# Second MoE of a fused attention and two-MoE kernel: one branch per pair of experts, and a second small product split by feature quarters

## The chip, the cores and the metric

The kernel runs on one core of a Trainium2 chip. The metric is the device time of one execution in microseconds (us); the time before is the median of three runs, 1041.02 us (1039.25 to 1041.88). Two times that lie within 0.3% of each other, some 3.1 us, are not told apart here.

## The reference, cut to what matters

A linear attention feeds a dense MoE (every token through all eight experts), and its output `x` (1152 tokens of 512 features) feeds a second MoE in which each token goes to one expert. Only that last part is touched:

```python
expert_idx = np.argmax(x @ w_gate, axis=1)          # one expert of E = 8 for each token
gate_w = probs[np.arange(N), expert_idx]
for i in range(N):                                   # capacity = 288 rows for each expert
    e = expert_idx[i]
    if counts[e] < capacity:
        disp[e, counts[e]] = x[i]; pos[i] = counts[e]; counts[e] += 1; keep[i] = True
h = np.maximum(np.einsum('ecd,edf->ecf', disp, w1), 0.0)   # D = 512, F = 1024
y = np.einsum('ecf,efd->ecd', h, w2)
out[i] = gate_w[i] * y[expert_idx[i], pos[i]]        # for the rows kept, else 0
```

How many rows an expert holds is known only when the kernel runs.

## The kernel before

The first 90% of the kernel (attention, first MoE, routing) ends with a scatter by GpSimd: each token's row of the tile `acc` (512 features and the gate weight and token number behind them) goes to its slot of the DRAM tensor `disp` (line 723). The rows of the first four experts' first 32 slots are also built on chip, as `xT`.

Then the second MoE runs expert by expert, `for e in range(E)`. It treats an expert's 288 slots in two parts.

- **The small part**, the first 32 slots, is always computed. `first_small` multiplies the 32 rows with w1 (16 matmuls, four of them side by side in the array's columns, each for a quarter of the 1024 features; 32 instructions in the trace, since a float32 matmul is issued as two). `relu_small` takes the result through ScalarE into `g`. `turn_small` transposes `g` on TensorE, VectorE copies it out as `h`. `second_small` multiplies with w2: 8 feature chunks times 4 quarters of the 512 outputs, 32 matmuls of 128 columns (64 instructions). `out_small` scales by the gate weight and GpSimd scatters the rows to `out`.
- **The large part**, slots 32 to 287, is computed only where an expert has more than 32 rows. A mask of those experts, `many`, is counted on chip, and each engine reads it into a register and branches on the expert's bit (lines 1171 and 1172). `large` splits the weights into a high part `hi` (ScalarE) and a low part left in place (VectorE), loads up to 256 rows (`rows_load`, on ScalarE's DMA queue), transposes and splits them into `xh` and `xl`, and runs two products of three matmuls each for every tile.

The order of one iteration, written out by hand for every engine: `turn_small(e)`, `out_small(e - 1)`, `first_small(e + 1)`, the branch, in it the large part or, in its Else, nothing of it, and in either arm `second_small(e)` (two copies of the same code), then `relu_small(e + 1)`, and the loads into the weight slots that expert e - 1 leaves (`done`, `load`). A weight piece has 512 KB, an expert has 8 pieces (four of w1, four of w2), and 36 slots hold them; SyncE's queue issues the loads in order. 36 pieces, up to the first half of expert 4, are loaded ahead of the loop.

The on-chip memory of this stage is a pool `yp` that opens over the tiles of the first MoE, `acc` among them: a tile that falls on the place of an old one waits until the old one's last reader is done. PSUM serves the small part from four banks in rotation (`bank2(0, ...)`) and the large part from four others.

Of the kernel before, what the change touches and what calls it, by code (L numbers as in the profile page):

```python
# [8 lines left out]
F32 = mybir.dt.float32  # L9
R32 = mybir.dt.float32r  # L10
# [10 lines left out]
def tile_linear_attention_two_moe(  # L21
# [68 lines left out]

    ident = const.tile([P, P], F32, name="ident")
    make_identity(nc, ident)
    ones = xp.tile([P, P], F32, name="ones")
    nc.vector.memset(ones, 1.0)
    ones_b = xp.tile([P, P], BF16, name="ones_b")
# [899 lines left out]
    def bank2(k, name):  # L995
        return psum2[k].tile([P, 512], F32, tag="ps", name=name)
# [8 lines left out]
    NQD = P // C0  # L1005
    DQ = D // NQD
    tails0 = yp.tile([P, E, RW - D], F32, name="tails0")
    part = yp.tile([P, 1], F32, name="part")
    where = yp.tile([P, E], I32, name="where")
    out_q = out.rearrange("n (j d) -> (n j) d", j=NQD)  # L1010

    def slots_load(p):
        xs = yp.tile([P, D], F32, tag="xs", bufs=1, name=f"xs_{p}")
        rows_of_slots(p, xs)
        return xs
# [6 lines left out]

    def rows_load(e, c0, n):
        xs = yp.tile([P, RW], F32, tag="xt", bufs=2, name=f"xs2_{e}_{c0}")
        nc.scalar.dma_start(xs[:n, :], disp[e * cap + c0 : e * cap + c0 + n, :])
        return xs

    def rows_out(o, at_, y, n):
# [8 lines left out]

    FP = F // NQD
    NH = FP // P

    def first_small(e):
        ps = bank2(0, f"q1_{e}")[:, :FP]
        x = xTs[e // EP]
        es = slice(e % EP * C0, (e % EP + 1) * C0)
        for c in range(DC):
            for j in range(NQD):
                js = slice(j * C0, (j + 1) * C0)
                nc.tensor.matmul(
                    ps[js], x[:, c, es], raws[e, c][:, 0, j * FP : (j + 1) * FP], start=c == 0, stop=c == DC - 1,
                    tile_position=(0, j * C0),  # L1050
                )
        return ps

    def relu_small(e, ps):
        g = yp.tile([P, FP], F32, tag="g", bufs=2, name=f"g_{e}")
        nc.scalar.activation(g, ps, AF.Relu)
        return g
# [7 lines left out]
        return h  # L1065

    def second_small(e, ps, h):
        for f in range(F // P):
            q, t = f // NH, f % NH
            for j in range(NQD):  # L1070
                js = slice(j * C0, (j + 1) * C0)
                nc.tensor.matmul(
                    ps[js], h[:, t, q * C0 : (q + 1) * C0], raws[e, DC + f // 2][:, f % 2, j * DQ : (j + 1) * DQ],
                    start=f == 0, stop=f == F // P - 1, tile_position=(0, j * C0),
                )

    def out_small(e, ps):
        y = yp.tile([P, DQ], F32, tag="y", bufs=3, name=f"y_{e}")
        nc.scalar.mul(y, ps, tails0[:, e, 0:1])
        rows_out(out_q, where[:, e : e + 1], y, P)  # L1080

    def large(e, chunks, rows, second):

        c0, w = chunks[0][0], sum(n for _, n in chunks)
        at_ = [c - c0 for c, _ in chunks]
# [10 lines left out]
        for c in range(0, DC, 2):  # L1096
# [4 lines left out]
                        ps[:, k, at_[i] : at_[i] + n], rows[i][:n, (c + k) * P : (c + k + 1) * P], ident[:n, :n]  # L1101
                    )
            split(xh[:, c : c + 2], xl[:, c : c + 2], ps)
        second()
        for i in range(1, DC):
            split_w(i)

# [34 lines left out]

    SETS = [REST[i : i + 2] for i in range(0, len(REST), 2)]
    assert len(SETS) <= 1
    xTs = {0: xT}
    xs = slots_load(1)
    for i in range(NQD):
        nc.sync.dma_start(
            tails0[i * C0 : (i + 1) * C0], disp[:, D:].rearrange("(e s) d -> s e d", e=E)[:C0]
        )  # L1150
    load(64)
    for j in range(NQD):
        nc.gpsimd.memset(part[j * C0 : (j + 1) * C0], float(j))
    g = relu_small(0, first_small(0))
    late = None
    for e in range(E):
        h = turn_small(e, g)
        if e == 0:
            wf = yp.tile([P, E], F32, name="wf")
            nc.vector.tensor_copy(wf, tails0[:, :, 1].bitcast(I32))  # L1160
            nc.vector.tensor_scalar(wf, wf, float(NQD), part[:, 0:1], ALU.mult, ALU.add)
            nc.vector.tensor_copy(where, wf)
        if e:
            out_small(e - 1, late)

        q = first_small(e + 1) if e + 1 < E else None
        late = bank2(0, f"q2_{e}")[:, :DQ]
        if REST:
            tc.no_sync_barrier()
            if e == 0:  # L1170
                mask = nc.values_load(many[0:1, 0:1], min_val=0, max_val=(1 << E) - 1)
            with tc.If(mask & (1 << e)) as more:  # L1172
                for chunks in SETS:
                    rows = [rows_load(e, c0, n) for c0, n in chunks]
                    large(e, chunks, rows, lambda: second_small(e, late, h))
            with more.Else():
                second_small(e, late, h)
        else:
            second_small(e, late, h)
        if q is not None:  # L1180
            g = relu_small(e + 1, q)
        if e % EP == 0 and e // EP + 1 < E // EP:
            xTs[e // EP + 1] = slots_copy(e // EP + 1, xqp, [slots_trans(e // EP + 1, xs)])
        if e:

            done(e - 1)
            load(64)
    out_small(E - 1, late)
    manual.close()


# [53 lines left out]
```

## Time and profile before

| | us |
|---|---|
| median of the runs | 1041.02 |
| lowest, highest | 1039.25, 1041.88 |
| the profiled execution, its own time | 1043.93 |
| its span, first to last instruction | 1042.2 |
| second MoE, from its first product to the end of the span | 144.1 |
| TensorE busy over the span | 988.1 (95%) |

The profiled execution is 2.9 us above the median. Busy time counts a matmul from start to modelled end; register, branch and DMA-issuing instructions are not counted as busy and are seen under an engine's queue (PEldq is TensorE's sequencer, SPq SyncE's). What stands in brackets behind an instruction is the idle time of its engine ahead of it and what ended it; "issue" means that the profile shows nothing that the engine waited for.

### The profile page before, as it was taken

To read this page: it belongs to the slowest core of one execution; us is meant where nothing else is said; L and a number is where in the kernel's file an instruction comes from. 1 tells how busy PE (TensorE), PEld (TensorE's weight loads), DVE (VectorE), ACT (ScalarE), POOL (GpSimd) and SP (SyncE) were. 2 spreads that over 40 slices of the span, in tenths; PEclk is the share of its full clock that TensorE was granted. 3 is DMA by queue.
4 is the path that set the end of the run, shared out by engine and by line. 5 is a ranking of instruction groups with operands and counts; after the bars stand their busy time and mean duration, and the time that the engine had idled before them with its cause. 6 is when DMAs were issued, how large, how long until landed. Compare 5 with 4: busy or idle time off the path is not lost. (4 is left out here: it accounts for less than half of the span.)

```text
span 1042.2 us, 17368 instructions
## 1 busy us (share of the span) xinstructions
PE 988.1 (95%) x6686; PEld 889.5 (85%) x6686; DVE 658.9 (63%) x1288; ACT 342.7 (33%) x768; POOL 455.2 (44%) x480
## 2 busy tenths in 40 slices
PE   7999999999999999999999999999999999658586
PEld 7999989889998899988998889998999888537465
DVE  6766699997666666666666666666666665314041
ACT  5766553323222232332222223232223212113031
POOL 3656887646544445455544444445553300200101
PEclk9999999999999999999999999999999999868998
DMA  8888789841111111111111111111111164685500
GB/s 261 279 280 276 248 296 329 310 152 61 41 42 41 41 42 41 60 43 60 43 42 42 41 41 41 43 60 46 56 41 62 61 212 173 213 299 170 189 25 27
DMA packets 59873, 125.73 MB, mean 121 GB/s; under 512 B 6969, under 2 KB 25789, under 8 KB 59264
## 3 DMA queue, kind: packets, MB, share of 16 engines
q1 hardware_dynamic: 57904, 120.72, 34.2%
q0 software_dynamic: 1296, 2.63, 0.7%
q8 instruction: 64, 1.05, 0.4%
q10 hardware_dynamic: 576, 1.07, 0.3%
q14 instruction: 33, 0.27, 0.1%
HBM read 114.61 MB, written 44.68 MB: 153 GB/s over the span
## 5 line engine op out<-in xcount | busy, mean ns | idle before, releaser
L81 POOL TENSOR_TENSOR l<-r,h 128x256 fp32r<-128x256 f32 (+2 forms) x100 | 155.1, 1566 | 335.7 <-ACT h L80 335.7
L614 DVE SCALAR_TENSOR_TENSOR acc<-p,prob,acc 128x512 f32<-128x512 f32 x252 | 188.3, 749 | 103.0 <-PE p L605 102.9
L605 PE MATMUL p<-h,hl 128*128 128x512 f32 x576 | 226.6, 393 | 0.0
L603 PE MATMUL p<-h,hh 128*128 128x512 f32 x576 | 226.3, 393 | 0.0
L604 PE MATMUL p<-l,hh 128*128 128x512 f32 x576 | 225.1, 391 | 0.0
L569 DVE TENSOR_TENSOR ca<-ca,p 128x256 f32<-128x256 f32 (+1 forms) x256 | 113.0, 450 | 69.9 <-PE p L552 67.5
L80 ACT CAST h<-r 128x256 fp32r<-128x256 f32 (+2 forms) x108 | 70.8, 685 | 180.3 <-PE p L605 159.3
L558 ACT ACTIVATE hh<-ca 128x320 fp32r<-128x320 f32 (+1 forms) x128 | 56.3, 443 | 223.0 <-DVE ca L569 223.0
L605 PEld LDWEIGHTS p<-h,hl 128*128 128x128 f32 x576 | 108.2, 188 | 23.5 <-DVE hl L562 0.2
L604 PEld LDWEIGHTS p<-l,hh 128*128 128x128 f32 x576 | 108.2, 188 | 21.7
L603 PEld LDWEIGHTS p<-h,hh 128*128 128x128 f32 x576 | 108.3, 188 | 20.4
L81 POOL TENSOR_TENSOR lt<-t,ht 128x256 fp32r<-128x256 f32 x144 | 124.3, 891 | 1.3 <-PE pn L352 1.3
L550 PE MATMUL p<-xh,ht 128*128 128x320 f32 x256 | 79.2, 309 | 0.0
L552 PE MATMUL p<-xh,lt 128*128 128x320 f32 x256 | 79.1, 309 | 0.0
L551 PE MATMUL p<-xl,ht 128*128 128x320 f32 x256 | 79.1, 309 | 0.0
L550 PE MATMUL p<-xs,ht 128*128 128x256 f32 x256 | 72.8, 284 | 0.0
L552 PE MATMUL p<-xs,lt 128*128 128x256 f32 x256 | 72.4, 283 | 0.0
L551 PE MATMUL p<-xs,ht 128*128 128x256 f32 x256 | 72.4, 283 | 0.0
L569 DVE TENSOR_TENSOR cb<-cb,p 128x320 f32<-128x320 f32 (+1 forms) x128 | 58.1, 454 | 18.9 <-PE p L552 18.1
L562 DVE SCALAR_TENSOR_TENSOR hl<-ca,hh 128x320 fp32r<-128x320 f32 (+1 forms) x128 | 63.3, 496 | 2.3 <-ACT hh L558 1.5
L219 POOL TENSOR_TENSOR t<-r 128x256 f32<-128x256 f32 x72 | 54.8, 783 | 22.5 <-DMA r<-w1a 21.9
L562 DVE SCALAR_TENSOR_TENSOR hl<-cb,hh 128x512 fp32r<-128x512 f32 (+1 forms) x64 | 53.8, 841 | 11.0 <-ACT hh L558 11.0
(234 smaller groups left out, 2032.4 us busy)
## 6 DMA issues: line engine op xcount, KB each, us to landing
rw<-wst SPq DMA_DIRECT2D x64, 512.0 KB, 5.6
r<-w1a SPq DMA_DIRECT2D x36, 512.0 KB, 3.5
r<-w2a SPq DMA_DIRECT2D x36, 512.0 KB, 3.5
wst<-w1b SPq DMA_DIRECT2D x32, 512.0 KB, 7.1
wst<-w2b SPq DMA_DIRECT2D x32, 512.0 KB, 7.7
disp<-acc SPq DMA_DIRECT2D x18, 260.0 KB, 4.9
v<-va SPq DMA_DIRECT2D x8, 325.0 KB, 3.9
rawq<-qT SPq DMA_DIRECT2D x8, 320.0 KB, 5.6
```

Source lines behind the costliest of these rows:

```text
L80: nc.scalar.copy(hi, src)
L81: (eng or nc.vector).tensor_tensor(lo, src, hi, ALU.subtract)
L550: nc.tensor.matmul(ps, ws_[0], xs[0], start=i == 0, stop=False)
L551: nc.tensor.matmul(ps, ws_[0], xs[1], start=False, stop=False)
L552: nc.tensor.matmul(ps, ws_[1], xs[0], start=False, stop=i == DI - 1)
L558: nc.scalar.activation(hv[:, q0 : q0 + 2 * src.shape[1] - 1 : 2], src, AF.Relu)
L562: nc.vector.scalar_tensor_tensor(lv[:, qs], src, 0.0, hv[:, qs], ALU.max, ALU.subtract)
L569: nc.vector.tensor_tensor(o, x, ps, ALU.add)
L603: nc.tensor.matmul(ps, a, w.w2[0][:, f, :], start=f == 0, stop=False)
L604: nc.tensor.matmul(ps, a, w.w2[1][:, f, :], start=False, stop=False)
L605: nc.tensor.matmul(ps, b_, w.w2[0][:, f, :], start=False, stop=f == FT - 1)
L614: nc.vector.scalar_tensor_tensor(o, ps, prob[:, t, e : e + 1], o, ALU.mult, ALU.add)
```

## The change

- **Branches.** The experts go in groups of two. Behind the small parts of both stands one branch on "either of the two is large"; inside it stand two branches, one for each expert, around `large`. There is no Else: the small part is straight code in front of the branch and is no longer inside any arm.
- **The second small product** takes a quarter of the features for each of the four column strips instead of a quarter of the outputs: 8 matmuls of 512 columns. Each strip then holds a partial sum of all 512 outputs. ScalarE copies it to `qa`, and one iteration later four matmuls with a constant `stack` (four 32 x 32 unit matrices on top of each other) add the four partial sums (`sum_small`). The constant is built by three VectorE additions at the start.
- **Rows ahead of weights.** `rows_load` moves from ScalarE's queue to SyncE's, where it stands ahead of the next weight loads. The slots of two experts are freed and refilled together, at the end of every second group on. `load(64)` and the first relu move ahead of `slots_load(1)`, whose four loads wait for the scatter.
- **Memory.** Five tiles `hi0` to `hi4` are allocated first in `yp`, so that what is allocated behind them falls elsewhere.

```diff
+    stack = const.tile([P, 32], F32, name="stack")
+    nc.vector.tensor_tensor(stack, ident[:, 0:32], ident[:, 32:64], ALU.add)
...
+    for k in range(5):
+        yp.tile([P, 2 * D], R32, tag=f"hi{k}", bufs=1, name=f"hi_{k}")
...
-        nc.scalar.dma_start(xs[:n, :], disp[e * cap + c0 : e * cap + c0 + n, :])
+        nc.sync.dma_start(xs[:n, :], disp[e * cap + c0 : e * cap + c0 + n, :])
...
     def second_small(e, ps, h):
-        for f in range(F // P):
-            q, t = f // NH, f % NH
+        for t in range(NH):
             for j in range(NQD):
                 js = slice(j * C0, (j + 1) * C0)
                 nc.tensor.matmul(
-                    ps[js], h[:, t, q * C0 : (q + 1) * C0], raws[e, DC + f // 2][:, f % 2, j * DQ : (j + 1) * DQ],
-                    start=f == 0, stop=f == F // P - 1, tile_position=(0, j * C0),
+                    ps[js], h[:, t, js], raws[e, DC + j][:, t, :], start=t == 0, stop=t == NH - 1,
+                    tile_position=(0, j * C0),
                 )
+        a = yp.tile([P, D], F32, tag="qa", bufs=1, name=f"qa_{e}")
+        nc.scalar.copy(a, ps)
+        return a
+
+    def sum_small(e, a):
+        ps = bank2(0, f"qs_{e}")[:, :DQ]
+        for j in range(NQD):
+            nc.tensor.matmul(
+                ps[j * C0 : (j + 1) * C0], stack, a[:, j * DQ : (j + 1) * DQ], start=True, stop=True,
+                tile_position=(0, j * C0),
+            )
+        return ps
...
-        second()
...
+    load(64)
+    g = relu_small(0, first_small(0))
     xs = slots_load(1)
...
     for e in range(E):
         h = turn_small(e, g)
+        q = first_small(e + 1) if e + 1 < E else None
+        if e:
+            late[e - 1] = sum_small(e - 1, a)
+        a = second_small(e, bank2(0, f"q2_{e}"), h)
+        if q is not None:
+            g = relu_small(e + 1, q)
...
         if e:
-            out_small(e - 1, late)
...
-            with tc.If(mask & (1 << e)) as more:
-                for chunks in SETS:
-                    rows = [rows_load(e, c0, n) for c0, n in chunks]
-                    large(e, chunks, rows, lambda: second_small(e, late, h))
-            with more.Else():
-                second_small(e, late, h)
...
+            out_small(e - 1, late.pop(e - 1))
...
+        if (e + 1) % GROUP == 0:
+            group = range(e + 1 - GROUP, e + 1)
+            if e + 1 == E:
+                out_small(e, sum_small(e, a))
...
+                with tc.If(mask & sum(1 << k for k in group)):
+                    for k in group:
+                        tc.no_sync_barrier()
+                        with tc.If(mask & (1 << k)):
+                            for chunks in SETS:
+                                large(k, chunks, [rows_load(k, c0, n) for c0, n in chunks])
+            if group[0]:
+                for k in group:
+                    done(k - GROUP)
+                load(64)
```

ScalarE, from the copy of `xT` that starts the second MoE to the first branch. Before (line 1056 is `relu_small`, lines 1171 and 1172 are the branch; DMASW are the scatter's completions):

```order
L907 COPY xT_9777<-xst_0_9657 128x256 [waits PE_49]
L1056 ACTIVATE g_9851<-q_0_9834 128x256 [waits DMASW3_49,DMASW4_49,DMASW2_49,DMASW5_49,DMASW1_49,DMASW6_49,DMASW0_49,DMASW7_49,DVE_49,PE_49]
L1171 TENSOR_LOAD many [waits DVE_49]
L1172 REGISTER_ALU
L1172 COMPARE_AND_BRANCH
```

ScalarE at the same place with the change (line 1065 is now `relu_small`, 1086 the copy to `qa`, 1101 the scaling of `out_small`, 1204 to 1208 the branches):

```order
L912 COPY xT_9781<-xst_0_9661 128x256 [waits PE_49]
L1065 ACTIVATE g_9847<-q_0_9830 128x256 [waits DVE_49,PE_49]
L1086 COPY qa_9893<-q_0_9884 128x512 [waits PE_49]
L1065 ACTIVATE g_9895<-q_1_9867 128x256 [waits DMASW4_49,DMASW3_49,DMASW5_49,DMASW2_49,DMASW6_49,DMASW1_49,DMASW7_49,DMASW0_49,DVE_49]
L1086 COPY qa_9933<-q_1_9924 128x512 [waits PE_49,Activation_49]
L1065 ACTIVATE g_9935<-q_2_9902 128x256
L1101 ACTIVATE y_9941<-qs_9919,tails_9818 128x128 [waits DMAHW5_49,DMAHW6_49,DMAHW4_49,DMAHW3_49]
L912 COPY xT_9951<-xst_9946 128x512 [waits PE_49]
L1204 TENSOR_LOAD many [waits DVE_49]
L1205 REGISTER_ALU
L1205 COMPARE_AND_BRANCH
```

The wait for the scatter has moved from the first `g` to the second, and a copy of the second product now stands ahead of every relu from expert 1 on.

TensorE, from the transposes of expert 0 to the first branch, before (line 1062 is `turn_small`, 1048 `first_small`):

```order
L1062 MATMUL ht_9853<-ident,g_9851 128x128 x2
L1048 MATMUL q_1_9862<-rw_0_9089,xT_9777 32x256 x4
L1048 MATMUL q_1_9862<-rw_1_9091,xT_9777 32x256 x4
L1048 MATMUL q_1_9862<-rw_2_9093,xT_9777 32x256 x4
L1048 MATMUL q_1_9862<-rw_3_9095,xT_9777 32x256 x4
L1171 TENSOR_LOAD many
L1172 REGISTER_ALU
L1172 COMPARE_AND_BRANCH
```

TensorE ahead of its first branch with the change, which now stands behind the small parts of experts 0 and 1 (1093 is `sum_small`, 1081 `second_small`, 1028 the transposes of the next four experts' rows):

```order
L1093 MATMUL qs_9919<-qa_9893,stack 32x128 x4
L1081 MATMUL q_1_9924<-rw_4_9101,h_9900 32x512
L1081 MATMUL q_1_9924<-rw_5_9103,h_9900 32x512
L1081 MATMUL q_1_9924<-rw_6_9105,h_9900 32x512
L1081 MATMUL q_1_9924<-rw_7_9273,h_9900 32x512
L1081 MATMUL q_1_9924<-rw_4_9101,h_9900 32x512
L1081 MATMUL q_1_9924<-rw_5_9103,h_9900 32x512
L1081 MATMUL q_1_9924<-rw_6_9105,h_9900 32x512
L1081 MATMUL q_1_9924<-rw_7_9273,h_9900 32x512
L1028 MATMUL xst_9946<-ident,xs_9849 128x128 x4
L1204 TENSOR_LOAD many
L1205 REGISTER_ALU
```

The second product has come out of the arms and stands as 8 matmuls of 512 columns ahead of the branch.

## Rows read from the trace of the kernel before

**Rows 1.** Busy time in stretches of the second MoE: engines, granted clock, DMA share, GB/s.

```profile
core 0: us, PE busy (x) PEld busy (x) DVE busy (x) ACT busy (x) POOL busy (x), PEclk, DMA share, GB/s
898.10:906.70 8.60, 1.93 (x32) 0.94 (x33) 0.95 (x5) 0.38 (x1) 3.54 (x8) 0.79 0.78 287
...
932.43:970.52 38.09, 31.31 (x254) 25.91 (x250) 14.16 (x16) 12.63 (x18) 1.02 (x2) 0.89 0.59 195
970.52:981.78 11.26, 5.69 (x98) 4.35 (x98) 0.86 (x2) 0.59 (x2) 2.87 (x3) 0.85 0.53 188
981.78:992.77 10.99, 5.82 (x103) 4.07 (x99) 0.42 (x1) 0.75 (x2) 0.97 (x1) 0.84 0.43 152
992.77:1001.11 8.34, 5.38 (x101) 3.86 (x99) 0.42 (x1) 0.75 (x2) 0.97 (x1) 0.85 0.04 9
1001.11:1031.05 29.94, 28.49 (x253) 23.95 (x251) 14.06 (x16) 12.54 (x18) 1.03 (x2) 0.98 0.06 20
1031.05:1042.20 11.15, 3.36 (x66) 2.39 (x66) 0.86 (x2) 0.57 (x2) 3.84 (x4) 0.73 0.17 61
```

**Rows 2.** Timeline (start, us, engine, line), the start of the second MoE.

```profile
901.18 0.98 POOL L723 DMA_INDIRECT disp<-acc,slot_i  x1 [0.30 <-issue]
906.26 0.38 ACT L1056 ACTIVATE g<-q 128x256 f32<-128x256 f32 x1 [8.22 <-DMA disp<-acc,slot_i]
909.94 1.70 SPq L535 DMA_DIRECT2D rw<-wst  x1
```

**Rows 3.** DMA traffic from 900 to 905 us.

```profile
DMA packets 701, 1.82 MB, mean 364 GB/s; under 512 B 197, under 2 KB 197, under 8 KB 701
```

**Rows 4.** Timeline of TensorE: small products and the idle time ahead of them.

```profile
907.32 3.16 PE L1048 MATMUL q<-rw,xT 128*32 128x256 f32 x32
...
970.89 1.93 PE L1048 MATMUL q<-rw,xT 128*32 128x256 f32 x32
978.39 3.46 PE L1072 MATMUL q<-rw,h 128*32 128x128 f32 x64 [5.57 <-issue]
981.78 0.44 PE L1062 MATMUL ht<-ident,g 128*128 128x128 f32 x2
...
998.03 3.15 PE L1072 MATMUL q<-rw,h 128*32 128x128 f32 x64 [2.96 <-issue]
```

**Rows 5.** TensorE's sequencer at the branch, single ones: duration in ns, start in us.

```profile
L1172 PEldq COMPARE_BRANCH  x1: 3828/3828/3828, 908.9 to 908.9; - x1
...
L1172 PEldq COMPARE_BRANCH  x1: 6758/6758/6758, 971.5 to 971.5; - x1
...
L1172 PEldq COMPARE_BRANCH  x1: 4042/4042/4042, 993.7 to 993.7; - x1
...
L1172 PEldq COMPARE_BRANCH  x1: 306/306/306, 1026.4 to 1026.4; - x1
...
L1172 PEldq COMPARE_BRANCH  x1: 461/461/461, 1031.1 to 1031.1; - x1
```

**Rows 6.** Timeline: a copy of 512 columns, and the first large expert.

```profile
920.99 0.59 ACT L907 COPY xT<-xst 128x512 f32<-128x512 f32 x1 [10.04 <-PE xst L1020]
...
934.21 1.05 ACT L80 CAST hi<-rw 128x1024 fp32r<-128x1024 f32 x1 [1.28 <-DVE h L1064]
935.29 1.23 DVE L81 TENSOR_TENSOR rw<-rw,hi 128x1024 fp32r<-128x1024 f32 x1 [1.71 <-ACT hi L80]
940.64 0.66 PE L1100 MATMUL xst<-ident,xs 128*128 128x128 f32 x2 [5.34 <-DMA xs<-disp]
947.44 0.38 PE L1113 MATMUL q<-xh,hi 128*128 128x256 f32 x1
```

**Rows 7.** Timeline of the end of the kernel.

```profile
1031.05 0.44 PE L1062 MATMUL ht<-ident,g 128*128 128x128 f32 x2 [0.35 <-ACT g L1056]
...
1032.28 0.98 POOL L1030 DMA_INDIRECT out<-y,xs  x1 [0.30 <-DVEq L1172]
...
1038.18 0.97 POOL L1030 DMA_INDIRECT out<-y,where  x1 [3.65 <-ACT y L1079]
```

More of the change, by code (lines that the diff above doesn't have):

```diff
@@ L92, in tile_linear_attention_two_moe @@
     make_identity(nc, ident)
+    stack = const.tile([P, 32], F32, name="stack")
+    nc.vector.tensor_tensor(stack, ident[:, 0:32], ident[:, 32:64], ALU.add)
+    nc.vector.tensor_tensor(stack, stack, ident[:, 64:96], ALU.add)
+    nc.vector.tensor_tensor(stack, stack, ident[:, 96:128], ALU.add)
     ones = xp.tile([P, P], F32, name="ones")
@@ L1039, in tile_linear_attention_two_moe @@
     NH = FP // P
+    assert C0 == stack.shape[1] and F // P // 4 == NH
     def first_small(e):
@@ L1080, in out_small, with large @@
         rows_out(out_q, where[:, e : e + 1], y, P)
-    def large(e, chunks, rows, second):
+    def large(e, chunks, rows):
         c0, w = chunks[0][0], sum(n for _, n in chunks)
@@ L1144, in tile_linear_attention_two_moe @@
     assert len(SETS) <= 1
+    GROUP = 2
     xTs = {0: xT}
+    load(64)
+    g = relu_small(0, first_small(0))
     xs = slots_load(1)
@@ L1150, in tile_linear_attention_two_moe @@
         )
-    load(64)
     for j in range(NQD):
         nc.gpsimd.memset(part[j * C0 : (j + 1) * C0], float(j))
-    g = relu_small(0, first_small(0))
-    late = None
+    late = {}
     for e in range(E):
         h = turn_small(e, g)
-        if e == 0:
+        q = first_small(e + 1) if e + 1 < E else None
[4 more added lines that the diff above has]
+            g = relu_small(e + 1, q)
+        if e == 1:
             wf = yp.tile([P, E], F32, name="wf")
@@ L1163, in tile_linear_attention_two_moe @@
         if e:
-            out_small(e - 1, late)
[L1166 to L1171, printed above, removed]
-            with tc.If(mask & (1 << e)) as more:
-                for chunks in SETS:
-                    rows = [rows_load(e, c0, n) for c0, n in chunks]
-                    large(e, chunks, rows, lambda: second_small(e, late, h))
-            with more.Else():
-                second_small(e, late, h)
[L1178 to L1182, printed above, removed]
-            xTs[e // EP + 1] = slots_copy(e // EP + 1, xqp, [slots_trans(e // EP + 1, xs)])
[L1184 to L1188, printed above, removed]
+            out_small(e - 1, late.pop(e - 1))
+        if e % EP == 1 and e // EP + 1 < E // EP:
+            xTs[e // EP + 1] = slots_copy(e // EP + 1, xqp, [slots_trans(e // EP + 1, xs)])
+        if (e + 1) % GROUP == 0:
+            group = range(e + 1 - GROUP, e + 1)
+            if e + 1 == E:
+                out_small(e, sum_small(e, a))
+            if REST:
+                tc.no_sync_barrier()
+                if group[0] == 0:
+                    mask = nc.values_load(many[0:1, 0:1], min_val=0, max_val=(1 << E) - 1)
+                with tc.If(mask & sum(1 << k for k in group)):
+                    for k in group:
+                        tc.no_sync_barrier()
+                        with tc.If(mask & (1 << k)):
[5 more added lines that the diff above has]
+                load(64)
     manual.close()
```

## The prediction

> **What bounds the kernel now.** I read the stretches of the second MoE first [rows 1]: the 144.1 us from 898.1 to the end of the span hold nine pieces, the wait at the start, one iteration for each expert and the tail. Two iterations are long, 38.1 and 29.9 us, for experts 2 and 6: only those two are large in this run. The others take 8 to 14 us although TensorE is busy for 5.4 to 5.8 us in the three listed (experts 3, 4, 5). TensorE is nonetheless what everything waits for: VectorE and ScalarE are busy less than 1 us of each. So the time to win is TensorE's idle time, and the timeline says where it lies. First, ScalarE's first relu waits until 906.26 for the scatter, 8.22 us [rows 2], because `g` lies over `acc`; TensorE is through with its first product at 900.0. Second, each second product of a small expert starts after idle time that no instruction ended, 5.57 us for expert 3 and 2.96 us for expert 5 [rows 4]. The sequencer's rows name it: its branch took 6.76 us at 971.5 and 4.04 us at 993.7, 3.83 us at 908.9 [rows 5]. All are branches that jump over the body. An arm that is entered costs next to nothing: only the jump past the Else at its end shows, 0.31 us. Third, expert 2's large part waits 5.34 us for its rows [rows 6], and the end is a small expert behind a large one, 11.15 us [rows 1].
>
> A rule of the Trainium skill speaks to the length of the jumps (Runtime: NRT & Kernel Launch, section Instruction fetch mechanics): a branch to a target outside the window of two fetched pages waits until the target's page has been fetched. By that rule a jump over two bodies costs what one over one body costs; by a price that grows with the distance two outer jumps would cost some 4 us more each. The trace has no jump over two bodies, only the equal bodies at 3.8 to 6.8 us, so it does not decide; the second price is in a rival below.
>
> **The change part by part.** I walk along TensorE with the new order, from 898.1, with durations from the rows.
>
> *Start.* The first product takes 1.93 (the full-clock price of 32 instructions, [rows 4]), relu 0.38, transposes 0.44, the next first product 1.93. The second product now has 16 instructions of 512 columns in place of 64 of 128: as many columns as a first product, so 1.93 at full clock and 3.16 at half [rows 4], where it took 3.15 to 3.46. TensorE reaches 905.0 without the scatter. But the second `g` still lies over `acc`: the wait moves by one expert and is not removed. The scatter's last issue is at 901.18 and its end was seen at 906.26. The two weight loads that stood behind it (909.94, [rows 2]) now go ahead, and the DMA was moving 364 GB/s then [rows 3], so 1.05 MB more can cost up to 2.9 us: the scatter lands between 906.3 and 909.2, I take 907.5. The next transposes start at 907.95: **9.85 us** from 898.1.
>
> *Rest of group 0.* Transposes, first product, sum, second product, four row transposes: about 5.4 us at full clock, 9 at half. After a pause the first product ran 3.16 us, not 1.93, so I take **7.85**. The sum is new, 8 instructions of 128 columns at 3.46 / 64 = 0.054: 0.45 us. Its own wait is nothing: the copy it reads was made an iteration earlier.
>
> *Outer branch of group 0, jumped.* The sequencer reaches a branch about 1.4 us ahead of the engine (971.5 against a first product that ends at 972.8, [rows 4, 5]). The jump took 3.83 and 4.04 us when few or no weights moved (0.04 of the DMA in expert 5's stretch) and 6.76 when they did (0.53) [rows 1, 5]. The weight loads stand behind this branch on SyncE, and so the queues are quiet: 4.0 - 1.4, plus reading the mask and a chance of a second page: **3.7**. Bounds: 0.5 (one jump took 0.46 [rows 5]) to 8.
>
> *Group 1.* Expert 2's small part: 4.75 us at full clock (0.44 + 1.93 + 0.45 + 1.93), 7.6 at half, I take 6.5. Then a **new wait**: ScalarE's copy of the second product, 0.59 us [rows 6], stands ahead of the relu (0.38) that the next transposes need, so TensorE stops about 1.0 us between the two experts of each group. Four such gaps replace branches; across a branch the copy is hidden by the jump. Expert 3: 5.0. Together **12.5**.
>
> *Large part of expert 2.* Its rows are loaded by SyncE once the first branch is past, some 10 us ahead of use: the 5.34 us go. What is late next is ScalarE: copy, relu and scaling (0.59 + 0.38 + 0.37), then the first `hi` (1.05) and a cast of 512 columns (0.59), then VectorE's low part of the rows, half of 1.23: 4.3 us until the first product can run, where before the small second product covered it. First product to the next transposes took 947.44 to 970.52, 23.1 us [rows 1, 6]. With 0.8 for a clock that has to come back: **28.2**. The branch over expert 3's body starts some 4.4 us before the end of this work (the end-of-arm jump at 1026.4 against 1030.7), so its 4 to 6.8 us are mostly covered: **1.0**.
>
> *Group 2:* 5.2 + 1.0 + 4.8 = **11.0**, its outer jump **3.4**. *Group 3:* 6.5 + 1.0 + 2.8 (expert 7 has no first product behind it) = **10.3**. *Large part of expert 6:* as before with the last sum and scaling ahead of it: **28.3**.
>
> *Tail.* Now the large part is last. Its second output is issued 1.6 us after TensorE's end (1032.28 against some 1030.7) and the last output landed 4.0 us after its issue at 1038.18 [rows 7]; with 0.7 for four times the bytes, **6.3**. The jump over expert 7's body is covered as above.
>
> Sum: 9.85 + 7.85 + 3.7 + 12.5 + 28.2 + 1.0 + 11.0 + 3.4 + 10.3 + 28.3 + 6.3 = 122.4, against 144.1: **-21.7 us**, a span of 1020.5. The profiled execution lies 2.9 above the median, so the difference goes on the median: 1041.0 - 21.7 = 1019.3. The three additions at the start and the changed order of weight loads in the first MoE cost nothing: VectorE is not the bound there, TensorE is, with its products always queued.
>
> **The rivals.**
>
> *Cheaper jumps.* If all three uncovered jumps cost 0.5, as one did, and the clock stays full, 3.2 + 2.9 + 1.0 and some 5 of half clock go: about 1007. One jump of six speaks for it.
>
> *Dearer jumps and a slow clock.* The jump pays by distance (4 more at each outer one) and each group starts and stays at half clock (2 more in each of four): about 1035 with a second page at one of them. The granted clock of 0.84 to 0.85 in the three short stretches [rows 1] speaks against half clock throughout.
>
> *Weights become the bound, and the kernel is slower.* Loads are now made in two lumps: 16 pieces once group 0 is past (919.5), 12 once expert 2's large part lets go. That is 14.7 MB until expert 7's second product at 984. Above 228 GB/s nothing waits. At 152 GB/s, the lowest of the stretches that still load [rows 1], the last piece comes 919.5 + 96.7 = 1016.2, some 32 late: 1051. It decides at 14.7 / 86.2 = 171 GB/s, where the 21.7 are lost. Against it: those stretches waited for slots, and where nothing held the queue it moved 364 [rows 3].
>
> *It does not do what it says.* The start is won by one expert only and the copy puts gaps where branches were; if every jump that is left shows in full (6.8, also behind both large parts' small ones) and the scatter lands at 909.2, 1.7 + 3.1 + 3.4 + 4.4 come back: about 1032, still faster.
>
> **How the numbers follow.** My forecast, 1011 to 1028: 0.74. Cheaper jumps, 1003 to 1011: 0.10. Dearer ones or the fourth case, 1028 to 1037: 0.10. Weights in part, no change: 0.02. Weights in full, slower: 0.04. The range leaves out the last two and the outer half of the two beside the forecast: 1008 to 1031. A difference of 0.3% (3.1 us) is what a measurement here can tell from none: faster 0.94, same 0.02, slower 0.04.
>
> **What would show it.** In the profile of the changed kernel: the second `g` (not the first) ends a wait for the scatter at 907 to 909; the sequencer shows two long branches without a large part ahead of them, 3.5 to 7 us each; the second product has 16 instructions in 1.9 to 3.2 us; transposes of the second expert of each group wait about 1 us for `g`; the large parts no longer wait for rows but 3 us for `xl`; expert 6's large part is last and ends some 6 us before the span. It would be wrong where a product waits for a weight load, where a jump over two bodies takes over 8 us, or where the large products run at the 1.2 GHz level for more than their first few us.

## The result and the profile after

The changed kernel takes 1026.57 us (median of four runs, 1024.65 to 1029.39) where the kernel before, run beside it, took 1040.13: a ratio of 0.987, with an interval of 0.984 to 0.990. The gain is 13.6 us; the forecast was 21.7, with 1019.3 us and a range of 1008 to 1031, in which the result lies. The profiled execution took 1026.11 us and has a span of 1024.3, 17.9 less than the one of before, which lay 2.9 above its median.

The span splits into two parts that went opposite ways. The second MoE begins at 906.77 (the first product of expert 0), not at 898.10: the work ahead of it, which the change hardly touches, became 8.67 us longer. From there to the end it takes 117.5 us; before it took 144.1, and the walk gave 122.4. So the part that was forecast gained 26.6 us, five more than forecast, and a third of that was lost in a place that the forecast had set to nothing.

First the second MoE in four stretches, for the kernel before: experts 0 and 1, then 2 and 3, then 4 and 5, then the rest (the columns are those of [rows 1]).

```profile
core 0: us, PE busy (x) PEld busy (x) DVE busy (x) ACT busy (x) POOL busy (x), PEclk, DMA share, GB/s
898.10:932.43 34.33, 17.62 (x233) 11.22 (x233) 2.38 (x10) 2.01 (x5) 4.51 (x9) 0.67 0.73 253
932.43:981.78 49.35, 37.00 (x352) 30.26 (x348) 15.02 (x17) 13.22 (x19) 3.89 (x4) 0.88 0.58 193
981.78:1001.11 19.33, 11.20 (x201) 7.93 (x197) 0.85 (x2) 1.50 (x4) 1.95 (x2) 0.85 0.27 90
1001.11:1042.20 41.09, 31.85 (x319) 26.34 (x316) 14.92 (x17) 13.11 (x19) 4.87 (x5) 0.92 0.09 31
```

The same four stretches of the changed kernel:

```profile
...
906.77:925.19 18.42, 12.46 (x144) 5.53 (x145) 2.35 (x10) 2.86 (x7) 4.05 (x8) 0.91 0.47 165
925.19:964.95 39.76, 35.48 (x268) 26.99 (x269) 14.48 (x17) 13.88 (x21) 2.19 (x4) 0.91 0.86 321
964.95:978.49 13.54, 8.76 (x117) 4.18 (x117) 1.10 (x3) 2.26 (x6) 3.65 (x4) 0.97 0.68 240
978.49:1024.30 45.81, 35.83 (x244) 26.46 (x244) 14.73 (x17) 14.06 (x21) 4.85 (x5) 0.87 0.08 27
```

The first three stretches gain 15.9, 9.6 and 5.8 us; the last one, with expert 6's large part, loses 4.7. TensorE is busy for 12.5 us of the first stretch in place of 17.6 although it makes as many columns and a sum: the granted clock there is 0.91, not 0.67. The transfers run at 321 GB/s in the second stretch and no product waits for a weight, so the rival of the weights falls. Expert 2's rows, 5.34 us late before [rows 6], are there in time; the large part waits 1.70 us for `xh` and 0.99 for `xl` in their place. The last output is issued at 1019.77 and the span ends 4.5 us later; before it was 4.0 [rows 7].

Now the timeline of the start (start, duration, engine, line, operation, idle time ahead and its releaser):

```profile
906.77 1.93 PE L1057 MATMUL q<-rw,xT 128*32 128x256 f32 x32
...
911.33 0.38 ACT L1065 ACTIVATE g<-q 128x256 f32<-128x256 f32 x1 [4.62 <-remote]
...
911.77 0.44 PE L1071 MATMUL ht<-ident,g 128*128 128x128 f32 x2 [3.07 <-ACT g L1065]
...
912.14 3.10 PE L1057 MATMUL q<-rw,xT 128*32 128x256 f32 x32
...
914.98 2.49 PE L1081 MATMUL q<-rw,h 128*32 128x512 f32 x16
...
915.14 1.71 SPq L905 DMA_DIRECT2D xs<-disp  x4
...
917.54 0.59 ACT L1086 COPY qa<-q 128x512 f32<-128x512 f32 x1 [5.83 <-PE q L1081]
918.02 0.39 ACT L1065 ACTIVATE g<-q 128x256 f32<-128x256 f32 x1
...
918.47 0.44 PE L1071 MATMUL ht<-ident,g 128*128 128x128 f32 x2 [0.99 <-ACT g L1065]
```

The last scatter has landed when SyncE loads what it wrote, at 915.14, 8.4 us after the start. The scatter held the first relu until 906.26 before [rows 2]; now the second relu was held not by it but by the copy of the partial sums, which stands ahead of it on ScalarE: the new wait of about 1.0 us that the prediction named, 0.99 here and 1.05, 1.02 and 1.06 in the other groups. The first relu begins at 911.33, 2.6 us after its product by the records; why, no run here tells. And the two uncovered jumps, now over two bodies, on TensorE's sequencer:

```profile
L1205 PEldq COMPARE_BRANCH  x1: 3346/3346/3346, 921.5 to 921.5; - x1
...
L1205 PEldq COMPARE_BRANCH  x1: 5439/5439/5439, 972.7 to 972.7; - x1
```

They left TensorE idle for 1.90 and 3.76 us:

```profile
925.19 0.41 PE L1071 MATMUL ht<-ident,g 128*128 128x128 f32 x2 [1.90 <-PEq L1205]
...
978.49 0.66 PE L1071 MATMUL ht<-ident,g 128*128 128x128 f32 x2 [3.76 <-PEq L1205]
```

Over one body the long ones had taken 3.8 to 6.8 us [rows 5]: the greater distance did not raise the price. That agrees with the rule of the Trainium skill (Runtime: NRT & Kernel Launch, section Instruction fetch mechanics) by which such a branch waits until its target's page is fetched; no run here shows the fetch itself.

### The profile page after: what moved, and what is told of

Read it like the earlier page. It is cut to its first block, busy times and chain, and to the rows that moved or that the text cites. A ratio compares the mean times of both kernels' runs of the same rounds, so it can differ in the third digit from the quotient of the medians.

```text
span 1024.3 us, 16761 instructions
## 1 busy us (share of the span) xinstructions
PE 991.1 (97%) x6366; PEld 878.0 (86%) x6366; DVE 659.7 (64%) x1291; ACT 346.0 (34%) x776; POOL 456.3 (45%) x480
## 4 chain that ended last, share of the span: by engine, by line
PE 73%; issue 14%; DMA 5%; POOL 4%; DVE 3%; ACT 1%; SPq 0%; POOLq 0%; another core or an unknown queue 0%; DVEq 0%
PE p L608 12%; PE p L610 11%; PE p L609 11%; PE p L555 10%; PE p L557 10%; PE p L556 10%; DMA disp<-acc,slot_i 3%; PE kvp L333 2%; PE pn L357 2%; POOL lt L81 1%; POOL l L81 1%; DMA out<-y,xs 1%; POOL out L1038 1%; PE qt L317 0%; PE pl L452 0%
## 5 line engine op out<-in xcount | busy, mean ns | idle before, releaser
L608 PE MATMUL p<-h,hh 128*128 128x512 f32 x576 | 229.2, 398 | 0.0
L609 PE MATMUL p<-l,hh 128*128 128x512 f32 x576 | 227.8, 395 | 0.0
L576 ACT COPY ca<-p 128x256 f32<-128x256 f32 (+1 forms) x64 | 25.2, 394 | 106.5 <-PE p L557 106.5
```

The source lines that it names most:

```text
L608: nc.tensor.matmul(ps, a, w.w2[0][:, f, :], start=f == 0, stop=False)
L609: nc.tensor.matmul(ps, a, w.w2[1][:, f, :], start=False, stop=False)
```

## Experiments: the 8.7 us ahead of the second MoE

The drift is even over the first MoE. In 300 to 800 us the step from the start of one product of the first layer to the next is 133 ns before and after (mean over more than 1,700 steps, products of 256 and of 320 columns together), but those of the second layer are 228.6, 228.2 and 230.5 ns before (by line) and 233.8, 233.3 and 233.0 after. There are 1,728 of these products, and so this is some 7 us. Their page lines (busy, mean ns of one) of the kernel before:

```profile
L605 PE MATMUL p<-h,hl 128*128 128x512 f32 x576 | 226.6, 393 | 0.0
...
L603 PE MATMUL p<-h,hh 128*128 128x512 f32 x576 | 226.3, 393 | 0.0
...
L604 PE MATMUL p<-l,hh 128*128 128x512 f32 x576 | 225.1, 391 | 0.0
```

and of the changed kernel, whose code is the same there:

```profile
L608 PE MATMUL p<-h,hh 128*128 128x512 f32 x576 | 229.2, 398 | 0.0
L609 PE MATMUL p<-l,hh 128*128 128x512 f32 x576 | 227.8, 395 | 0.0
L610 PE MATMUL p<-h,hl 128*128 128x512 f32 x576 | 227.8, 395 | 0.0
```

The new matrix `stack` takes 128 bytes of each partition among the constants, and every pool behind it lies 128 bytes higher, `hh` and `hl`, the stationary operands of these products, among them. Against this stood the changed order of SyncE's weight loads, or a slow execution.

**128 bytes more, and nothing else.** The kernel before with

```diff
+    pad = const.tile([P, 32], F32, name="pad")
+    nc.vector.memset(pad, 0.0)
```

> The kernel before with one constant tile more, 128 bytes in each partition, that no later instruction reads; it sits where the change puts its matrix of four stacked identities, so that the tiles of the pools behind it lie 128 bytes higher, and nothing else differs. The change's profile shows the second MoE beginning 8.7 us later than before, gained evenly over the first MoE, and nearly all of it in that MoE's second products (512 columns each: 228.6, 228.2 and 230.5 ns from one start to the next before, 233.8, 233.3 and 233.0 after; 1728 of them, about 7.3 us). Theory P (placement): the hidden halves that these products read lie 128 bytes higher, and that alone does it. P expects some 7 us more than before (1047 us), steps of 233 ns in the second products of the first MoE, and the second MoE beginning near 905. Theory D (the execution, or the order of SyncE's weight loads, which the change moves and this kernel does not): the same time as before within 1.5 us, steps of 229 ns, beginning at 898.

Measured: 1046.64 us, a ratio to before of 1.0044 (1.0027 to 1.0061), the second MoE beginning at 906.29, steps of 233.8, 233.3 and 233.0 ns. Its row for the first of the three lines is that of the changed kernel:

```profile
L605 PE MATMUL p<-h,hh 128*128 128x512 f32 x576 | 229.2, 398 | 0.0
```

P holds and D falls. The time grew by less than the 8.2 us that the start moved: the second MoE took 138.7 us in this profile, 5.4 less, among other things through shorter jumps (5.57 us idle ahead of expert 3's second product before, 3.68 here).

**512 bytes.** The changed kernel with 384 bytes of padding.

> The changed kernel with 384 bytes more of unused constants in each partition, so that the pools behind lie 512 bytes higher than before the change, not 128. Theory P in its stricter form (what counts is where the operand lies within some power of two of bytes): the 7 us come back, 1019 us, steps of 229 ns in the second products of the first MoE. P in its looser form (the old place happened to be good and any other is worse): no gain, 1026. Theory D (order of the weight loads, or the execution): 1026.6, steps of 233.

Measured: 1019.72 us, 0.9788 (0.9761 to 0.9814), steps of 228.5, 228.3 and 230.6, beginning at 899.13. The strict form of P holds: the place within some power of two counts.

**Only the hidden halves.** In the kernel of the tree alone (below; 1010.3 us), 128 bytes ahead of `hh` and `hl` and 384 behind.

```diff
+    hpool.tile([P, 32], F32, name="pad_h")
...
+        if not padded:
+            padded.append(hpool.tile([P, 96], F32, name="pad_x"))
```

> The tree with the old second product (1010.3 us, steps of 228.5 ns in the first MoE's second products) with the hidden halves hh and hl alone 128 bytes higher: 128 bytes of unused space ahead of them and 384 behind, so that every tile behind lies 512 bytes higher, which cost nothing in the run with 512, and `acc` and the constants lie where they lay. Theory P1 (it is where TensorE's stationary operand begins): steps of 233 ns, some 7 us more, 1017. Theory P2 (it is where VectorE's sums in `acc`, the constants or the tiles of the first layer lie, through what other engines do beside the products): 228.5 and 1010.

Measured: 1015.65 us, 5.3 more than without, and steps of 233.8, 233.3 and 233.0. It is the place of these two tiles, not what lies around them:

```profile
L608 PE MATMUL p<-h,hh 128*128 128x512 f32 x576 | 229.2, 398 | 0.0
```

**Which places.** The tree alone with 352 and with 256 bytes of padding.

> The tree with the old second product (1010.3 us) with 352 bytes of unused constants, so that the hidden halves, the stationary operand of the first MoE's second products, begin on a multiple of 512 bytes in each partition. They begin 160 bytes behind one in the kernel before (steps of 228 ns), 288 behind in the change and in the run with 128 bytes more (233), 160 again in the run with 512 more (228). Theory A (the grid is best): steps below 228, at the least 213.3 (512 columns at 2.4 GHz), so up to 1728 x 15 ns = 26 us less. Theory B (two levels, some places are bad): 228 or 233, so 1010 or 1017.

> The tree with the old second product with 256 bytes of unused constants, so that the hidden halves begin 416 bytes behind a multiple of 512. So far 160 bytes behind one was good (228.5 ns), 288 and 0 were bad (233). Theory R256 (what counts is the place within 256 bytes: 160 good, 32 and 0 bad): steps of 228.5, 1010 us. Theory R512 (the place within 512 bytes): 233, 1017, or a third level.

Measured: 1016.75 us and 233.4, 233.2 and 232.7 ns with 352; 1008.92 us and 228.6, 228.2 and 230.6 with 256. Their rows, 352 first:

```profile
L606 PE MATMUL p<-h,hh 128*128 128x512 f32 x576 | 228.9, 397 | 0.0
```

```profile
L606 PE MATMUL p<-h,hh 128*128 128x512 f32 x576 | 226.4, 393 | 0.0
```

So there are two levels, and the place within 256 bytes separated them. By the addresses in the programs, three places 160 bytes behind a multiple of 256 are good, and one place each 32 and 0 bytes behind one is bad; 160 and 32 lie 128 bytes apart, so the place within 128 bytes would not separate them. A start on the grid is not the good place. The Trainium skill (SBUF — State Buffer, section Specifications (TRN2)) knows lines of 16 bytes; all these places are multiples of 32, and so that rule would make no difference between them. What in the chip makes it, these runs do not show. The records of the weight loads last 188 ns at both levels, and the runs do not separate TensorE's reads of the two tiles from the writes of ScalarE and VectorE into them.

## Experiments: the new second product

**The tree without it.** The changed kernel with the old second product of 64 instructions, no copy, no sum and no `stack`:

```diff
-        for t in range(NH):
+        for f in range(F // P):
...
-            late[e - 1] = sum_small(e - 1, a)
-        a = second_small(e, bank2(0, f"q2_{e}"), h)
+        late[e] = bank2(0, f"q2_{e}")[:, :DQ]
+        second_small(e, late[e], h)
```

> The tree of branches, the late output of each small expert and the weight order of the changed kernel, but the small second product as it was before: 64 instructions of 128 columns, no copy of partial sums, no sum by a product, and no matrix of stacked identities, so that the pools lie where they lay before. From the rows of the change: its eight second products take 17.5 us and would take some 27.5 (+10.0); its sums take 3.9 us (gone); the four gaps behind the copy 4.1 (gone), one wait for the last copy 0.8 (gone); copies ahead of the two large parts 1.2 (gone). So the second MoE itself comes out the same, 117.5 us, within 2. Theory P (placement of the hidden halves slows the first MoE by 7.3 us): 1019.3 us, steps of 229 ns, the second MoE beginning at 899. Theory D (order of the weight loads in the first MoE, which this kernel keeps): 1026.6, beginning at 907.

Measured: 1010.30 us, 0.9687 (0.9661 to 0.9712), steps of 228.6 ns, beginning at 897.38. The loss ahead is gone with the order of the weight loads kept, as P has it. But the second MoE itself did not stay the same; it took 111.3 us, 6.2 less than in the change:

```profile
...
897.38:918.97 21.59, 13.57 (x232) 8.71 (x233) 2.37 (x10) 1.99 (x5) 4.47 (x9) 0.81 0.50 170
918.97:954.71 35.74, 34.68 (x348) 28.18 (x348) 14.56 (x17) 13.01 (x19) 2.07 (x3) 0.92 0.94 351
954.71:967.27 12.56, 8.32 (x197) 5.91 (x197) 1.21 (x3) 1.28 (x4) 3.75 (x4) 0.92 0.78 276
967.27:1008.70 41.43, 32.78 (x316) 26.98 (x316) 14.74 (x17) 13.11 (x19) 4.86 (x5) 0.91 0.10 30
```

The 10 us expected from dearer second products were wrong: the old form takes 1.93 us at full clock, the new one 1.90.

```profile
901.94 1.93 PE L1076 MATMUL q<-rw,h 128*32 128x128 f32 x64
```

The first stretch is 3.2 us longer than in the changed kernel (its second relu waits for the scatter), the third 1.0 shorter, and the two with a large part are 4.0 and 4.4 shorter. Of the 4.4, 3.1 lie in group 3's small parts (the gap and the sum of expert 7 among them) and 1.3 in expert 6's large part and the tail. ScalarE in the changed kernel, ahead of expert 2's large part (TensorE's second product runs from 934.47 to 936.3):

```profile
936.49 0.59 ACT L1086 COPY qa<-q 128x512 f32<-128x512 f32 x1 [4.15 <-PE q L1081]
936.97 0.39 ACT L1065 ACTIVATE g<-q 128x256 f32<-128x256 f32 x1
...
937.50 1.05 ACT L80 CAST hi<-rw 128x1024 fp32r<-128x1024 f32 x1
...
938.43 1.09 ACT L80 CAST xh<-xst 128x512 fp32r<-128x512 f32 x2
...
940.47 0.58 PE L1134 MATMUL q<-xl,hi 128*128 128x256 f32 x1 [0.99 <-DVE xl L81]
```

and with the old product, which runs from 927.65 to 929.5:

```profile
927.96 0.38 ACT L1060 ACTIVATE g<-q 128x256 f32<-128x256 f32 x1 [3.99 <-PE q L1052]
...
928.49 1.05 ACT L80 CAST hi<-rw 128x1024 fp32r<-128x1024 f32 x1
...
930.25 1.07 ACT L80 CAST xh<-xst 128x512 fp32r<-128x512 f32 x2 [0.71 <-ACT hi L80]
...
931.61 0.38 PE L1116 MATMUL q<-xl,hi 128*128 128x256 f32 x1 [0.34 <-DVE xl L81]
```

With the old product the relu and the first cast run beside it, and the large part is ready 2.1 us after it. With the copy in front, they wait for the end of the product, the large part is ready 4.2 us after it, and its first products then run at the 1.2 GHz level (0.41 us each at 941, at a granted clock of 0.50; 0.28 from 943.5 on, at 1.00).

**The relu ahead of the copy.**

```diff
-        a = second_small(e, bank2(0, f"q2_{e}"), h)
+        ps2 = second_small(e, bank2(0, f"q2_{e}"), h)
         if q is not None:
             g = relu_small(e + 1, q)
+        a = part_small(e, ps2)
```

> The changed kernel with ScalarE's two instructions in the other order within each group of two: the relu of the next expert goes ahead of the copy of this expert's partial sums. The profile of the change shows TensorE idle 0.99, 1.05, 1.02 and 1.06 us behind that relu, once in each group; the prediction put this gap on the copy (0.59 us) that stands ahead of it. Theory: the four gaps go nearly whole, about 4 us, to 1022.5 us, and the copy, which is only read one expert later, makes nothing wait, but for expert 7, whose sum comes right behind (0.76 us now). Rival: what is late is the relu itself and the product ahead of it (the relu waits for the last instruction of the first product, whose end is seen late), so the gaps shrink by half at most: 1024.5 or more.

Measured: 1018.94 us, 0.9784 (0.9753 to 0.9816). The gaps are gone in groups 1 to 3; in group 0 the second relu waits for the scatter in place of the copy, and TensorE stands 2.58 us. Some 3.6 us more went than expected, and not behind the gaps, where the changed kernel's products had run at the full-clock price (1.93 us). In this execution the second MoE began 0.9 us earlier, the first relu was on time, and the products behind the first jump ran at full clock (1.93 us for the first product of group 1, 2.84 in the change). The rows tie some 3 us, the three gaps, to the order itself. The large part's own stretch stayed at 28.4 us (931.82 to 960.24; 28.65 in the change), since the copy still stands ahead of the casts, at 932.01.

**The copy on VectorE**, with 512 bytes of offset.

```diff
-        nc.scalar.copy(a, ps)
+        nc.vector.tensor_copy(a, ps)
```

> The changed kernel in the good place (512 bytes, 1019.7 us in the run with that alone) with the copy of the partial sums on VectorE in place of ScalarE. Theory: the copy on ScalarE costs by its place in the order, not by its 0.59 us: relu, scaling and the first two casts of a large part stand behind it and so behind the end of the second product, where with the old second product they ran beside it (the first cast at 937.50 behind a second product that ends at 936.3, against 928.49 ahead of 929.5). On VectorE nothing is queued behind it that is needed soon. So four gaps of 1.0 us go and each of the two large parts starts some 3.4 us earlier (28.6 us against 25.2 with the old second product): 1019.7 - 4.1 - 6.8 = 1009, within 3. Rival: the large parts start late for another reason (the half clock of their first products, or the product ahead that is shorter in the new form): only the gaps go, 1015.5.

Measured: 1010.50 us, 0.9715 (0.9697 to 0.9734), against 1009 expected. Expert 2's large part takes 25.7 us, the cast begins at 924.86, under the second product (924.24), and the four gaps are gone:

```profile
924.24 1.90 PE L1083 MATMUL q<-rw,h 128*32 128x512 f32 x16
...
924.86 1.05 ACT L80 CAST hi<-rw 128x1024 fp32r<-128x1024 f32 x1
...
926.20 0.69 DVE L1088 COPY qa<-q 128x512 f32<-128x512 f32 x1 [3.14 <-PE q L1083]
```

So moving the copy out of ScalarE's order gave back 9.2 us, although it takes longer on VectorE (0.69 against 0.59 us): its place had cost, not its duration. One part of the expectation failed: for expert 6, the time from the transposes of its rows to the end of the span fell only from 34.8 us in the run with 512 bytes to 33.7, since the sum of expert 7, which needs the copy, still stands ahead of its casts. And the new second product with all this mended is worth no more than the old one (1010.5 against 1010.3).

**The new second product in the old loop**, with its copy behind the relu and the same 512 bytes.

```diff
-            out_small(e - 1, late)
+            out_small(e - 1, sum_small(e - 1, a))
...
             g = relu_small(e + 1, q)
+        a = part_small(e, late)
```

> The kernel before with one part of the change alone, the small second product by quarters with its copy and its sum, in the old loop of one branch for each expert; the copy stands behind the next relu on ScalarE so that it makes no gap, and 384 bytes of unused constants go with the stacked identities so that the pools behind lie 512 bytes higher, a place that costs nothing by the run with 512. Theory C (columns): the 16 instructions of 512 columns take what the 64 of 128 columns took at the same clock (1.90 against 1.93 us at full clock in the rows of the change and of the tree alone), so nothing is won and eight sums of 0.40 to 0.68 us come on top: 1042 + 4 = 1046 us. Theory N (number of instructions, which the prediction used when it set 1.93 to 3.16 beside 3.15 to 3.46): 1.3 us less in each of eight, 4 us more for the sums: 1036.

Measured: 1038.22 us, 0.9982 (0.9963 to 1.0001), between the two, and by its interval not told apart from the kernel before. The prices are those of theory C, the old 1.93 and 3.64 us at granted clocks of 1.00 and 0.50 (the first two lines; the third is another case, see below):

```profile
916.81 1.92 PE L1078 MATMUL q<-rw,h 128*32 128x512 f32 x16 [2.04 <-DVE wf L1181]
...
927.40 3.64 PE L1078 MATMUL q<-rw,h 128*32 128x512 f32 x16 [5.41 <-issue]
...
971.50 3.24 PE L1078 MATMUL q<-rw,h 128*32 128x512 f32 x16
```

The total missed C by 8 us. All second products together, before and here (busy us, mean ns of one, idle us ahead of and between them):

```profile
L1072 PE MATMUL q<-rw,h 128*32 128x128 f32 x512 | 26.3, 372 | 26.8 <-issue 23.8 <-DVE wf L1160 2.4 <-DVEq L1172 0.6
...
L1078 PE MATMUL q<-rw,h 128*32 128x512 f32 x128 | 22.0, 782 | 15.5 <-issue 13.1 <-DVE wf L1181 2.0 <-DVEq L1193 0.3
```

The busy time fell by 4.3 us at the same prices, so with the granted clock, and the idle time by 11.3. Two stalls in the middle of the 64 instructions (3.08 and 2.48 us before, ended by no instruction) have no counterpart. The jump at expert 3 left no idle time where it had left 5.57; but the product behind it took 3.24 us at a granted clock of 1.00 (971.50), its weight loads with pauses of up to 0.60 us that no instruction ended. By these rows, of one execution each, the shorter code saved time at the branches, not at the products; why one jump takes 0.34 us and the next 6.2, no run here tells.

## Experiments: the tree and the start

**One branch for each expert** in the kernel of the tree alone, the inner branch taken out with it.

```diff
-    GROUP = 2
+    GROUP = 1
```

> The tree with the old second product, with one branch for each expert in place of the tree, and everything else of the change kept (small parts ahead of the large part, late output, rows by SyncE, the start). Five jumps are then uncovered where the tree has two (3.39 and 2.96 us idle in its trace): three more at 3 to 5 us each, the half clock of 1 to 3 us behind each, and at the end expert 7's small part, 6 us, behind the large part of expert 6 with its jump. Theory (the tree is the main gain): 1010.3 + 10 + 5 + 5 = 1030, between 1024 and 1036. Rival (the main gain is the start and the order of the large parts; jumps are cheap, as one of none and one of 0.46 us show): below 1020.

Measured: 1019.14 us, 0.9807 (0.9755 to 0.9858): the rival's side of 1020. The uncovered jumps left some 8.7 us idle, hardly more than the tree's 6.8. The largest loss is one wait, of expert 2's large part for its rows:

```profile
916.56 5.56 SPq L536 DMA_DIRECT2D rw<-wst  x8
...
922.47 0.86 SPq L1029 DMA_DIRECT2D xs<-disp  x2
...
931.34 2.13 PE L1104 MATMUL xst<-ident,xs 128*128 128x128 f32 x8 [10.68 <-DMA xs<-disp]
```

SyncE issues the rows behind eight weight loads that a finished expert set free. In the tree no slot comes free before group 1's branch, so the rows go first and nothing waits. The tree is worth 8.8 us, and by these rows the larger part of that is the order of rows and weights, not the number of jumps. That one branch each with the rows ahead would be as fast as the tree is argued, not tried.

**The start.** The tree alone with six large buffers set aside in place of five, so that no `g` lies over `acc`, and with none, as in the kernel before.

> The tree with the old second product (1010.3 us) with one more of the large experts' buffers set aside ahead of the small tiles, six in place of five, so that neither `g` nor `part` lies over `acc` any more. With five, the relu of expert 1 and the first memset of `part` waited for the last scatter of the rows (907.56 and 907.52, 7.80 us idle), TensorE stood 4.13 us and the next two products ran at half clock (3.64 and 2.96 us against 1.93). Theory: the wait goes, and what is late next is the load of the second half of the rows, which reads what the scatter writes and is needed 6.9 us after the relu: 4.1 us of waiting and up to 2.7 of half clock come back, of which the rows give back some 1 to 3: 1005 to 1008. Rival: the scatter is only met one step later (the rows, or the first scaling) and nothing moves: 1010.

> The tree with the old second product without the buffers of the large experts set aside ahead of the small tiles, so that `g` of both first experts lies over `acc` again as in the kernel before. The first relu then waits for the last scatter in place of the second one; expert 1's first product and expert 0's second product come behind the wait, 1.93 each at full clock, up to 3.6 each at half. Theory (the prediction's start term): 4 to 6 us more, 1014 to 1016. Rival (the wait only moves, as the run with six buffers gained nothing): 1010 to 1012.

Measured: 1009.89 us with six and 1010.90 with none, against 1010.30 with five. The three lie within 0.3% of each other, so both stand with their rivals. With none, the wait for the scatter sits at 908.17 on the copy of `h` and the second relu together, and TensorE stands 6.51 us ahead of the second product in place of 4.13 ahead of the transposes:

```profile
908.17 0.38 ACT L1057 ACTIVATE g<-q 128x256 f32<-128x256 f32 x1 [8.38 <-DMA disp<-acc,slot_i]
908.18 0.42 DVE L1065 COPY h<-ht 128x256 f32<-128x256 f32 x1 [9.71 <-DMA disp<-acc,slot_i]
```

With six it is gone, but the first relu begins late (902.59, 3.80 us idle on TensorE) and a later jump took 5.23 us, not 2.96. Group 0 ends 2.2 us earlier with six and 2.3 later with none, and the clock and the jumps behind give both back.

## Why the prediction was right and wrong

- **Faster, by waits and jumps:** right in sum. The tree alone, without the new second product, gave 31.7 us (1041.97, the kernel before run beside it, to 1010.30). How these divide among the start, the jumps and expert 2's rows is shown in two places only: one branch for each expert in place of the tree loses 8.8 us, and taking the first `g` off `acc`, by which the forecast moved the wait for the scatter, is worth 0.6, not told apart from nothing. In the changed kernel 117.5 us stand against 122.4 forecast. Start: 11.7 for 9.85 (the first relu's delay and the copy); in the run with 512 bytes 10.8, with the second relu held by the scatter until 909.52, as forecast. Rest of group 0: 4.8 for 7.85, since the clock stayed full. Outer jumps as idle time with reading the mask: 1.9 and 3.8 for 3.7 and 3.4. Inner jump: 0.5 for 1.0. Groups 1 to 3: 11.2, 9.8 and 11.1 for 12.5, 11.0 and 10.3. Large parts: 28.0 and 28.6 for 28.2 and 28.3. Tail: 6.1 for 6.3.
- **The step that failed** is the sentence that "the three additions at the start ... cost nothing". As work they cost nothing that the runs show; the 128 bytes of their result cost some 7 us by where they push the hidden halves. Together with about one microsecond of other drift that is the 8.7 us, and without it the kernel takes 1019.7 us, the forecast to half a microsecond. That closeness is partly luck: in the profiled execution of the run with 512 bytes the second MoE took 116.7 us, 5.7 less than forecast, and that execution lay 2.0 us below its median where the one of before lay 2.9 above.
- **A step that was right by cancelling:** the second product. The text noted that its columns stay the same and then set 1.93 or 3.16 us beside 3.15 to 3.46, as if the old one had that price at any clock. At equal clock the prices are equal. Nor is 3.16 the half-clock price: that product met both levels (granted clock 0.59), and at 0.50 it takes 3.64 (928.86 in the kernel before). What was gained there is clock, which the tree alone gains too.
- **A step right in size and not followed:** the copy. The gaps of 1.0 us and the 28.2 us of the large part were forecast to a few tenths, the 4.3 us of preparation included (4.1 measured, though the terms listed for it add up to only 3.6). The text did not ask what the old second product would have left: 25.2 us for expert 2. The new second product thus cost 9 us in the good place and 16 in the bad one, and the tree alone beats the changed kernel with 1010.3 us.
- **Rivals:** dearer jumps by distance fell (3.3 and 5.4 us over two bodies); weights as the bound fell (321 GB/s and no wait, where it needed under 171); cheaper jumps fell for the outer ones; jumps shown in full (the fourth) fell, with 1.9, 3.8 and 0.5 us idle.

## What to carry over

A constant tile that is added, taken away or resized moves everything allocated behind it; compare the mean duration of products that the change does not touch, and if it moved, pad back to the old place before judging the change. An instruction put on an engine costs what is queued behind it: ask which later work used to run beside the operation that it now waits for. Fewer and wider products with the same columns won nothing here in their own price (1.90 to 1.92 against 1.93 us at full clock); compare prices only at the same granted clock.

## What the runs showed of the hardware that was not expected

- The place of a stationary operand within 256 bytes of its partition changes the pace of 128x128 by 512 products in this kernel between 229.1 and 233.4 ns (mean of the three lines, 1.9%), with the same two levels, within 0.5 ns, in the fourteen traces (five places in all); it costs 5 to 7 us of 1010.
- A jump over a body on TensorE took between 0.3 and 6.8 us in these kernels, and one branch repeats its price only roughly: in six kernels with the code of the tree alone the first outer jump left 3.18 to 3.53 us idle and the second 2.92 to 5.23. The price goes with what the DMA engines do meanwhile: of the 40 jumps of more than 1 us in the fourteen traces, the 15 during which these were busy for less than 10% of the time took 1.5 to 4.0 us, and all 16 of 4.5 us or more fell where they were busy for 35% or more. Seven shorter ones fell there too, so this is a link and not a shown cause.
- Behind a pause, small products ran at the 1.2 GHz level again and again (3.64 us at a granted clock of 0.50 in place of 1.93 at 1.00); in six kernels 2.58 to 4.38 us of waiting for the scatter cost a further 1.5 to 3.0 us in the products behind.
